# An attention-plus-MLP kernel: score tiles of three and two heads in turn, VectorE's scores beside them, shared PSUM banks, filler matmuls

## The chip, the cores and the metric

One core of a Trainium2 chip. Times are device microseconds (us) of one execution. A run of one core is called slow when it lies over 1.5% above the fastest run of the same kernel in its session. The other runs are called fast. "Half clock" below is a granted TensorE clock of 0.50 in the records; full is 1.00.

## The reference, cut to what matters

Sequence 2048, width 512, 32 heads of 16. The result gates two branches that read the same input `x`:

```python
g = sigmoid((x * gate_w).sum(-1, keepdims=True))
q, k, v = heads(x @ wqkv)                        # (cut) 32 heads of 16
p = softmax((q @ k.T) * 16 ** -0.5)              # 2048 x 2048 for each head
a = merge(p @ v) @ wo
h = gelu(layernorm(x) @ w1)                      # (cut) then shifted along the sequence in four quarters
x1 = x + shifted(h) @ w2
b = x1 + gelu(layernorm(x1) @ w3) @ w4           # 512 -> 1792 -> 512
out = g * a + (1 - g) * b
```

The exponentials dominate: 32 heads of 2048 x 2048. With keys on the partitions this is 2048 blocks of 128 x 512.

## The kernel before

The kernel walks 32 groups: four chunks `c` of 512 queries by eight sets `g` of four heads. A group has 16 key tiles `kt` of 128 keys. In 13 of them ScalarE takes the exp. In the other three (`DKT`) VectorE approximates it: one op per head turns a score into integer bits (`kb`), and four adds make shifted copies (`sj`), which enter the value product as bf16. I call one such key tile a VectorE unit.

Contraction is over 32 rows, so a score matmul takes one of four row groups of the array, and matmuls on different row groups overlap ("row" passes: in the trace of before, at half clock, two together take 0.61 us, as long as one full-array matmul). Value products use four column groups ("col" passes: four together take 0.62 us). Everything else uses the full array.

```python
DKT = (4, 9, 14)
T_ALL = 880.0                                     # sets how fast the schedule hands out the side work
...                                               # (cut)
ps_act = tile_pool(name="ps_act", bufs=2, space=PSUM)    # 2 x 2 banks: exp's scores
ps_dve = tile_pool(name="ps_dve", bufs=1, space=PSUM)    # 1 bank: VectorE's scores
ps_acc = tile_pool(name="ps_acc", bufs=1, space=PSUM)    # 1 bank: the group's value product
ps_gen = tile_pool(name="ps_gen", bufs=2, space=PSUM)    # 2 banks: projections, MLP
...
def qk_a(n):                                      # two heads of one key tile
    c, g, kt, hf = a_tiles[n]
    stage[n] = st = ps_act.tile([P, 1024], F32, tag="sa", name="sa")
    for j in range(2):
        scores(st[:, j * 512:(j + 1) * 512], c, g, kt, 2 * hf + j)

def exp_a(n):
    pts[n] = pt = ptpool.tile([P, 1024], BF16, tag="pt", name="pt")
    nc.scalar.activation(out=pt[:], in_=stage.pop(n)[:], func=ACT.Exp, scale=LN2 / 128.0)
...
def qk_d(h):                                      # one head for VectorE
    st[h] = ps_dve.tile([P, 512], F32, tag="sd", name="sd")
    scores(st[h][:], c, g, kt, h)

def k_op(h):
    nc.vector.tensor_scalar(out=sj[0][:, h * 512:(h + 1) * 512], in0=st.pop(h)[:],
                            scalar1=KB, scalar2=0.0, op0=ALU.add, op1=ALU.max)
```

A list scheduler in the kernel's Python fixes the order on every engine before the program exists. It weighs exps first and puts projections, VectorE units and MLP into the gaps by due times.

The softmax here doesn't subtract the row's maximum and nothing guards it: scores larger than these inputs give would overflow.

Of the kernel before, what the change touches and what calls it, by code (L numbers as in the profile page):

```python
# [26 lines left out]
POOL_J = ()  # L27
DKT = (4, 9, 14)
PTB = 7
KPB = 2  # L30
SPB = 5
T_ALL = 880.0
# [33 lines left out]
class Task:  # L66
    def __init__(self, sched, engine, cost, fn, deps, due, mode, take, give, lat, qk):
        self.sched, self.engine, self.cost, self.fn, self.due, self.mode = sched, engine, cost, fn, due, mode
        self.take, self.give, self.lat, self.qk = take, give, lat, qk
        self.deps, self.done, self.blocked = deps, Event(), 0  # L70
        for d in deps:
            if d.t is None:
                d.waiters.append(self)
                self.blocked += 1
        if not self.blocked:
            sched.ready[engine].append(self)
        sched.left += 1


class Scheduler:  # L80
# [9 lines left out]
    TOL = 0.12  # L90

    def __init__(self, t0):
        self.ready = {e: [] for e in self.LAT}
        self.free = {e: t0 for e in self.LAT}
        self.mode, self.left = None, 0
        self.busy = {e: 0.0 for e in self.LAT}

    def add(self, engine, cost, fn, deps=(), due=0.0, mode=None, take=(), give=(), lat=None, qk=False):
        t = Task(self, engine, cost, fn, list(deps), due, mode, take, give, self.LAT[engine] if lat is None else lat, qk)
        return t.done  # L100
# [12 lines left out]
    def pick(self, e):  # L113
        t, best = self.free[e], None
        cands = []
        qk = None
        for k in self.ready[e]:
            s = self.start_of(k, t)
            if s is None:
                continue  # L120
            if k.qk:
                if qk is None or k.due < qk[1].due:
                    qk = (s, k)
            else:
                cands.append((s, k))
        if e == "PE" and qk is not None:
            limit = qk[0] + self.TOL
            cands = [(s, k) for s, k in cands if s + k.cost + (self.SWITCH if k.mode != self.mode else 0.0) <= limit]
            cands.append(qk)
        if not cands:  # L130
            return None
# [3 lines left out]

    def run(self):
        while self.left:
            picks = [(p[0], e, p[1]) for e in self.LAT if self.ready[e] and (p := self.pick(e)) is not None]
            s, e, k = min(picks, key=lambda p: p[0])
            self.emit(s, e, k)  # L140

    def emit(self, s, e, k):
        self.ready[e].remove(k)
        for r in k.take:
            r.take()
        cost = k.cost
        if e == "PE" and k.mode != self.mode:
            cost += self.SWITCH
            self.mode = k.mode
        self.now = s  # L150
        k.fn()
        self.left -= 1
        self.busy[e] += cost
        self.free[e] = s + cost
        for r in k.give:
            r.give(s + cost + k.lat)
        k.done.set(s + cost + k.lat)
# [3 lines left out]
def kernel(  # L161
# [28 lines left out]
    AKT = [t for t in range(NT) if t not in DKT]  # L190
    ND, NA = len(DKT), len(AKT)

# [6 lines left out]
    ps_act = ctx.enter_context(tc.tile_pool(name="ps_act", bufs=2, space=bass.MemoryType.PSUM))  # L199
    ps_dve = ctx.enter_context(tc.tile_pool(name="ps_dve", bufs=1, space=bass.MemoryType.PSUM))  # L200
# [13 lines left out]
    NVA, NVD = NA * H * VW, ND * H * VW  # L214
# [12 lines left out]
    junk = work.tile([P, D], BF16, tag="ot", name="junk")  # L227
    djc = const.tile([P, max(1, len(POOL_J))], I32, name="djc")

# [26 lines left out]
    for k, j in enumerate(POOL_J):  # L256
        nc.vector.memset(djc[:, k:k + 1].bitcast(I16), DJ[j])

    T0 = 13.0
    sc = Scheduler(T0)  # L260
    add = sc.add
    gen_s, acc_s, act_s, dve_s = Slots(2), Slots(1), Slots(2), Slots(1)
    pt_s, k_s, sj_s, q_s, xn_s, xnT_s = Slots(PTB), Slots(KPB), Slots(SPB), Slots(2), Slots(2), Slots(1)
    accsb_s, bcs_s, oTg_s, oT_s, ot_s = Slots(2), Slots(1), Slots(1), Slots(2), Slots(2)
    MM, DV, DV4, DV2 = 0.216, 0.69, 0.43, 0.43

    def gen_tile(dt=F32):
        return ps_gen.tile([P, 512], dt, tag="gen", name="gen")


    def mm_group(pairs, evacs, deps, due, n=512, ev_due=0.5, take0=()):
# [8 lines left out]
        for i, (a, b) in enumerate(pairs):  # L280
            prev = add("PE", MM * n / 512, lambda i=i, a=a, b=b: mm(i, a, b), list(deps) + ([prev] if prev else []) if i == 0 else [prev],
                       due, "full", take=(gen_s,) + tuple(take0) if i == 0 else (), lat=None if i == len(pairs) - 1 else 0.0)
        for i, (cost, fn, take, give) in enumerate(evacs):
            prev = add("DVE", cost, lambda fn=fn: fn(box["ps"]), [prev], due + ev_due, take=take,
                       give=tuple(give) + ((gen_s,) if i == len(evacs) - 1 else ()))
        return prev

    def transposes(src, dst, deps, due, give=()):
        box = {}

        def pe():
            box["ps"] = ps = gen_tile(BF16)
            for kt in range(KT):
                nc.tensor.transpose(ps[:, kt * P:(kt + 1) * P], src()[:, kt * P:(kt + 1) * P], ident[:])  # L294

        e = add("PE", 0.25, pe, deps, due, "full", take=(gen_s,), give=give)
        return add("DVE", DV2, lambda: nc.vector.tensor_copy(out=dst(), in_=box["ps"][:].rearrange("p (k t) -> p k t", k=KT)),
                   [e], due + 0.5, give=(gen_s,))


    PER = (T_ALL - T0 - 15.0) / (NCH * NG * 2 * NA)

    def when(c, g, kt=0.0):
        return T0 + ((c * NG + g) * 2 * NA + 2 * NA * kt / NT) * PER
# [7 lines left out]
    k_ev = {(0, 0): Event(T0)}  # L312
    q_ev = {(0, 0): Event(T0)}
# [4 lines left out]
    def project_k(g, c, due):  # L318
        k_ev[(g, c)] = mm_group(
            [(wkv[:, 0, kt, P * g:P * g + P], xT[:, kt, c * 512:(c + 1) * 512]) for kt in range(KT)],  # L320
            [(DV, lambda ps: nc.vector.tensor_copy(out=kT[g][:, c * 512:(c + 1) * 512], in_=ps[:]), (), ())],
            xT_ev[4 * c:4 * c + 4], due)

    def q_evac(g, c, ps, par):
        if par == 0:
            qm[(g, c)] = work.tile([P, 2, 512], BF16, tag="qT", name="qT")
        nc.vector.tensor_scalar(out=qm[(g, c)][:, par, :], in0=ps[:], scalar1=qmask[:, par:par + 1], scalar2=None,  # L327
                                op0=ALU.mult)

    def project_q(g, c, due):  # L330
        q_ev[(g, c)] = mm_group(
            [(wq[:, kt, P * g:P * g + P], xT[:, kt, c * 512:(c + 1) * 512]) for kt in range(KT)],
            [(DV, lambda ps: q_evac(g, c, ps, 0), (), ()), (DV, lambda ps: q_evac(g, c, ps, 1), (), ())],
            xT_ev[4 * c:4 * c + 4], due, take0=(q_s,))

    def v_evac(t, h0, nh, j, ps):
        src = ps[:, 0:nh * DH].rearrange("p (h d) -> p h d", h=nh)
        if t in AKT:
            nc.vector.tensor_copy(out=vpA[:, AKT.index(t), h0:h0 + nh, 1:VW], in_=src)
            return  # L340
        dst = vpD[j][:, DKT.index(t), h0:h0 + nh, :]
        nc.vector.tensor_scalar(out=dst[:, :, 1:VW], in0=src, scalar1=CJ[j], scalar2=None, op0=ALU.mult)

    def project_v(t, half, due):
        h0, nh = 16 * half, 16
        v_ev[(t, half)] = mm_group(
            [(xT[:, kt, t * P:(t + 1) * P], wkv[:, 1, kt, h0 * DH:(h0 + nh) * DH]) for kt in range(KT)],
            [(0.43, lambda ps, j=j: v_evac(t, h0, nh, j, ps), (), ()) for j in range(1 if t in AKT else NJ)],
            xT_ev[t:t + 1], due, n=nh * DH)

    for c in range(1, NCH):
# [3 lines left out]
    for t in range(NT):  # L355
        project_v(t, 1, when(0, 4) - 60.0 + 3.0 * t)
    for c in range(NCH):
# [8 lines left out]
    cg = [(c, g) for c in range(NCH) for g in range(NG)]  # L366
    a_tiles = [(c, g, kt, hf) for c, g in cg for kt in AKT for hf in range(2)]
    nA = len(a_tiles)
    stage, pts = {}, {}
    accs = {}  # L370
    left = {k: NA + ND * NJ for k in cg}
    q_use = {}
    for c, g in cg:
        q_use[(g // 2, c)] = q_use.get((g // 2, c), 0) + NA * 2 + ND * 4
# [11 lines left out]
    d_next = {"n": 0}  # L386
    d_units = []

    def qk_a(n):
        c, g, kt, hf = a_tiles[n]  # L390
        stage[n] = st = ps_act.tile([P, 1024], F32, tag="sa", name="sa")
        for j in range(2):
            scores(st[:, j * 512:(j + 1) * 512], c, g, kt, 2 * hf + j)
        q_done(g // 2, c)

    def exp_a(n):
        pts[n] = pt = ptpool.tile([P, 1024], BF16, tag="pt", name="pt")
        nc.scalar.activation(out=pt[:], in_=stage.pop(n)[:], func=ACT.Exp, scale=LN2 / 128.0)  # L398
# [61 lines left out]
    for n, (c, g, kt, hf) in enumerate(a_tiles):  # L460
        t = T0 + n * PER
        e = add("PE", 0.226, lambda n=n: qk_a(n), [k_ev[(g // 2, kt // 4)], q_ev[(g // 2, c)]], n, "row", take=(act_s,), qk=True)
        exp_ev.append(add("ACT", 0.9625, lambda n=n: exp_a(n), [e], t, take=(pt_s,), give=(act_s,)))
        if hf == 1:
            pv_ev[(c, g)].append(add(
                "PE", MM, lambda n=n, k=(c, g), kt=kt: pv(k, kt, AKT.index(kt) * H * VW, lambda i: (
                    pts[n - 1 + i // 2][:, (i % 2) * 512:(i % 2 + 1) * 512])),
                exp_ev[-2:] + [v_ev[(kt, g // 4)]] + pv_ev[(c, g)][:1], t + 3.0, "col",
                take=(acc_s,) if kt == AKT[0] else (), give=(pt_s, pt_s), lat=-MM if kt == AKT[0] else None))
# [4 lines left out]
    for c, g in cg:  # L474
        for x, kt in enumerate(DKT):
            t0 = when(c, g, (x + 0.3) * NT / ND) - LEADT
# [5 lines left out]
            def qk_d(h, c=c, g=g, kt=kt, st=st):  # L482
                st[h] = ps_dve.tile([P, 512], F32, tag="sd", name="sd")
# [3 lines left out]
            def k_op(h, st=st, sj=sj):  # L487
                if h == 0:
# [4 lines left out]
            def add_op(j, sj=sj):  # L493
                sj[j] = spool.tile([P, 2048], I16, tag="sj", name="sj")
                if j in POOL_J:
                    nc.gpsimd.tensor_add(sj[j][:].bitcast(I32), sj[0][:].bitcast(I32),
# [284 lines left out]
```

## Time and profile before

| | before |
|---|---|
| median, runs | 974.91 us; 973.31 to 982.2 (4 runs) |
| profiled span | 978.9 us, mean clock 0.906 |
| busy: TensorE, ScalarE, VectorE | 890.6, 832.9, 727.8 us |

From the page of before, part 1 (busy us, share of the span, instructions) and three lines of part 2 (the span in 40 slices; `PEclk` is the granted clock in tenths):

```profile
PE 890.6 (91%) x6632; PEld 262.7 (27%) x6730; DVE 727.8 (74%) x1286; ACT 832.9 (85%) x906; POOL 57.5 (6%) x42
...
DVE  2898899989998883468878477887656888845652
ACT  1647877899998986699999899999889999979990
...
PEclk7888999999999985599999699999689999959985
```

No engine is saturated from end to end. ScalarE has holes early, and drops to 6 to 8 tenths wherever `PEclk` falls to 5 or 6. The next answer is of the same trace in 20-us windows; its columns are the window, its length, the busy us (and instructions) of TensorE, its weight loads, VectorE, ScalarE and GpSimd, then clock, DMA share and GB/s:

```profile
core 0: us, PE busy (x) PEld busy (x) DVE busy (x) ACT busy (x) POOL busy (x), PEclk, DMA share, GB/s
40.00:60.00 20.00, 16.85 (x117) 7.17 (x113) 17.64 (x44) 5.82 (x6) 0.00 (x0) 0.71 0.00 1
60.00:80.00 20.00, 17.53 (x122) 5.93 (x123) 16.84 (x45) 11.80 (x13) 0.00 (x0) 0.83 0.01 2
360.00:380.00 20.00, 18.90 (x86) 3.45 (x86) 7.03 (x13) 13.62 (x15) 0.00 (x0) 0.50 0.01 2
380.00:400.00 20.00, 19.53 (x103) 3.37 (x100) 7.88 (x13) 12.90 (x13) 1.26 (x1) 0.50 0.05 17
420.00:440.00 20.00, 19.25 (x158) 5.75 (x159) 15.13 (x25) 20.00 (x23) 1.28 (x1) 1.00 0.06 18
```

There are three regimes. At 40–80 VectorE is 84 to 88% busy and ScalarE starves. At 360–400 the clock is 0.50, TensorE is 95 to 98% busy and ScalarE gets 13 to 14 of 20 us. At 420 the clock is full and ScalarE runs without a hole. ScalarE's timeline in the second and third regime (start, length, instructions merged, and in brackets the idle time before and what ended it):

```profile
350.10 1.28 ACT L644 ACT_TABLE_LOAD   x1
351.39 7.40 ACT L644 ACTIVATE g2T<-g2T 128x512 bf16<-128x512 bf16 x14
358.81 1.28 ACT L398 ACT_TABLE_LOAD   x1
...
366.95 1.02 ACT L398 ACTIVATE pt<-sa 128x1024 bf16<-128x1024 f32 x1 [0.48 <-PE sa L383]
368.58 1.02 ACT L398 ACTIVATE pt<-sa 128x1024 bf16<-128x1024 f32 x1 [0.60 <-PE sa L383]
...
417.54 33.51 ACT L398 ACTIVATE pt<-sa 128x1024 bf16<-128x1024 f32 x36 [0.22 <-PE sa L383]
```

Gelu (`g2T`) and its two table loads occupy 10 us. Then exps come about 1.5 us apart, nearly all singly and most of them waiting for `PE sa`, until 417; after that 36 follow in 33.51 us. TensorE in the slow regime:

```profile
366.25 0.61 PE L383 MATMUL sa<-qT,kT 32*128 32x512 bf16 x2
366.78 0.62 PE L408 MATMUL acc<-pt,vp 128*32 128x512 bf16 x4
367.33 0.61 PE L612 MATMUL gen<-w,g2T 128*128 128x512 bf16 x1
367.87 0.61 PE L383 MATMUL sa<-qT,kT 32*128 32x512 bf16 x2
368.41 1.03 PE L612 MATMUL gen<-w,g2T 128*128 128x512 bf16 x2
369.38 0.61 PE L383 MATMUL sa<-qT,kT 32*128 32x512 bf16 x2
```

Each pass of a new kind starts 0.54 us after the last, and a second of the same kind 0.42 us. From one score tile to the next it takes 1.5 to 1.6 us, more than the 0.93 us of an exp. ScalarE's waits in total (us, times, longest):

```profile
ACT pt L398 <- PE acc L408: 54.7, 38, 7.1
...
ACT pt L398 <- PE sa L383: 44.3, 64, 4.7
```

### The profile page before, as it was taken

How to read it: one execution, taken by the hardware profiler on the slowest of the kernel's cores; microseconds unless marked ns; L12 is line 12 of the kernel's file. 1: busy time of each engine (PE TensorE's matmuls, PEld its weight loads, DVE VectorE, ACT ScalarE, POOL GpSimd, SP SyncE). 2: the span in 40 equal slices, each digit the busy share in tenths (PEclk: the TensorE clock that was granted, in tenths of full speed). 3: DMA queues.
4: the chain of work that ended last, by engine and by line, in shares of the span. 5: the costliest groups of instructions: out<-in, count | busy, mean ns of one | idle time of the engine just before them, and what ended most of it. 6: DMA issues, size and time to landing. Idle time of an engine off the chain costs nothing.

```text
span 978.9 us, 17077 instructions
## 1 busy us (share of the span) xinstructions
PE 890.6 (91%) x6632; PEld 262.7 (27%) x6730; DVE 727.8 (74%) x1286; ACT 832.9 (85%) x906; POOL 57.5 (6%) x42
## 2 busy tenths in 40 slices
PE   4879999999999989999999999999899999899982
PEld 1332333322232221122222222222222222212220
DVE  2898899989998883468878477887656888845652
ACT  1647877899998986699999899999889999979990
POOL 5000000000000000000000000000000000000000
PEclk7888999999999985599999699999689999959985
DMA  7000000020020000001000000000000100000001
GB/s 220 1 1 16 15 3 15 15 90 15 14 90 10 16 10 15 1 16 37 15 15 16 15 13 22 31 15 14 5 15 15 32 20 17 12 4 16 15 16 36
DMA packets 27953, 23.52 MB, mean 24 GB/s; under 512 B 12000, under 2 KB 23136, under 8 KB 27872
## 3 DMA queue, kind: packets, MB, share of 16 engines
q1 hardware_dynamic: 27072, 21.64, 7.1%
q8 instruction: 52, 0.85, 0.4%
q10 hardware_dynamic: 800, 0.79, 0.2%
q14 instruction: 29, 0.24, 0.1%
HBM read 17.69 MB, written 2.62 MB: 21 GB/s over the span
## 4 chain that ended last, share of the span: by engine, by line
PE 50%; ACT 30%; issue 9%; DVE 9%; DMA 1%; SPq 0%; POOLq 0%; ACTq 0%; DVEq 0%
ACT pt L398 26%; PE sa L383 16%; PE acc L408 14%; PE gen L612 7%; PE gen L595 5%; PE sd L383 4%; DVE sj L499 4%; PE gen L277 3%; ACT g2T L644 2%; DVE kb L490 2%; PE gen L294 1%; ACT hT L644 1%; DVE qT L327 1%; ACT L398 1%; DMA bcs<-rd 0%
## 5 line engine op out<-in xcount | busy, mean ns | idle before, releaser
L398 ACT ACTIVATE pt<-sa 128x1024 bf16<-128x1024 f32 x832 | 780.7, 1062 | 104.0 <-PE acc L408 54.7
L383 PE MATMUL sa<-qT,kT 32*128 32x512 bf16 x1664 | 345.5, 403 | 32.4 <-ACT pt L398 25.3
L490 DVE TENSOR_SCALAR kb<-sd 128x512 int16<-128x512 f32 x384 | 263.2, 685 | 125.0 <-PE sd L383 112.8
L499 DVE TENSOR_SCALAR sj<-kb 128x2048 int16<-128x2048 int16 x384 | 264.2, 726 | 1.9
L383 PEld LDWEIGHTS <-kT 32*128 32x128 bf16 x2048 | 103.4, 92 | 332.4 <-issue 321.8
L408 PE MATMUL acc<-pt,vp 128*32 128x512 bf16 x1664 | 166.4, 408 | 0.3 <-ACT pt L398 0.3
L383 PE MATMUL sd<-qT,kT 32*128 32x512 bf16 x384 | 152.4, 397 | 7.4 <-DVE kb L490 5.4
L408 PE MATMUL acc<-sj,vp 128*32 128x512 bf16 x1536 | 149.0, 414 | 5.2 <-DVE sj L499 4.6
L408 PEld LDWEIGHTS <-vp 128*32 128x32 bf16 x3584 | 75.9, 96 | 181.8 <-issue 173.5
L441 POOL TENSOR_TENSOR oTg<-accsb,bcs 128x512 bf16<-128x512 f32 x32 | 43.9, 1372 | 907.3 <-DMA bcs<-rd 645.7
L595 PE MATMUL gen<-xnT,w 128*128 128x512 bf16 x252 | 81.0, 385 | 1.6 <-issue 1.4
L612 PE MATMUL gen<-w,g2T 128*128 128x512 bf16 x194 | 76.7, 472 | 3.1 <-issue 3.1
L602 DVE CAST g2T<-gen 128x512 bf16<-128x512 f32 x56 | 38.4, 686 | 15.0 <-PE gen L595 12.2
L420 DVE COPY accsb<-acc 128x512 f32<-128x512 f32 x32 | 22.0, 689 | 27.5 <-issue 20.4
L408 PE MATMUL acc<-kb,vp 128*32 128x512 bf16 x384 | 40.5, 413 | 0.3 <-issue 0.3
L595 PEld LDWEIGHTS <-w 128*128 128x128 bf16 x288 | 21.8, 97 | 49.8 <-issue 44.7
L612 PE MATMUL gen<-wo,oT 128*128 128x512 bf16 x58 | 20.1, 434 | 15.2 <-DMA oT<-oTg 14.6
L612 PEld LDWEIGHTS <-g2T 128*128 128x128 bf16 x224 | 17.1, 103 | 46.6 <-issue 42.8
L644 ACT ACTIVATE g2T<-g2T 128x512 bf16<-128x512 bf16 x56 | 29.6, 616 | 0.0
L719 DVE TENSOR_TENSOR x_sb<-x_sb,gen 128x512 bf16<-128x512 bf16 x16 | 11.0, 686 | 24.6 <-PE gen L612 21.2
L327 DVE TENSOR_SCALAR qT<-gen,qmask 128x512 bf16<-128x512 f32 x32 | 23.7, 744 | 4.2 <-PE gen L743 3.0
L687 DVE TENSOR_TENSOR dd<-gen,x_sb 128x512 f32<-128x512 f32 x16 | 11.0, 688 | 17.1 <-PE gen L612 17.0
(68 smaller groups left out, 336.9 us busy)
## 6 DMA issues: line engine op xcount, KB each, us to landing
bcs<-rd SPq DMA_DIRECT2D x32, 256.0 KB
w<-in_B_w_dram SPq DMA_DIRECT2D x2, 1792.0 KB
oT<-oTg SPq DMA_DIRECT2D x128, 16.0 KB, 1.8
out_dram<-ot SPq DMA_DIRECT2D x16, 128.0 KB, 2.3
x_sb<-in_A_x_dram SPq DMA_DIRECT2D x3, 512.0 KB
w<-in_B_w_dram SPq DMA_DIRECT2D x2, 512.0 KB
wq<-in_A_wqkv_dram SPq DMA_DIRECT2D x1, 512.0 KB
wkv<-in_A_wqkv_dram ACTq DMA_DIRECT2D x1, 512.0 KB, 7.2
```

Of the source, the lines that this page charges most:

```text
L277: nc.tensor.matmul(box["ps"][:, 0:n], lhsT=a, rhs=b, start=(i == 0), stop=(i == len(pairs) - 1))
L327: nc.vector.tensor_scalar(out=qm[(g, c)][:, par, :], in0=ps[:], scalar1=qmask[:, par:par + 1], scalar2=None, op0=ALU.mult)
L383: nc.tensor.matmul(dst, lhsT=kT[g // 2][r:r + 32, kt * P:(kt + 1) * P], rhs=qm[(g // 2, c)][r:r + 32, g % 2, :], start=True, stop=True, ti ...
L398: nc.scalar.activation(out=pt[:], in_=stage.pop(n)[:], func=ACT.Exp, scale=LN2 / 128.0)
L408: nc.tensor.matmul(accs[k][32 * i:32 * i + 32, :], lhsT=vp[:, v:v + 32], rhs=parts(i), start=first, stop=left[k] == 0, skip_group_check=Tr ...
L441: nc.gpsimd.tensor_tensor(out=box["o"][:], in0=box["a"][:], in1=box["b"][:], op=ALU.mult)
L490: nc.vector.tensor_scalar(out=sj[0][:, h * 512:(h + 1) * 512], in0=st.pop(h)[:], scalar1=KB, scalar2=0.0, op0=ALU.add, op1=ALU.max)
L499: nc.vector.tensor_scalar(out=sj[j][:], in0=sj[0][:], scalar1=float(DJ[j]), scalar2=None, op0=ALU.add)
L595: nc.tensor.matmul(outs["ps"][:], lhsT=w()[:, i, m * P:(m + 1) * P], rhs=box["xnT"][:, i, :], start=(i == 0), stop=(i == KT - 1))
L602: return e, add("DVE", DV, lambda: nc.vector.tensor_copy(out=dst(), in_=outs["ps"][:]), [e], at + 0.5, give=(gen_s,))
L612: nc.tensor.matmul(outs["ps"][:], lhsT=a, rhs=b, start=(i == 0), stop=(i == len(pairs) - 1))
L644: nc.scalar.activation(out=t[:, m, n0:n1], in_=t[:, m, n0:n1], func=ACT.Gelu_apprx_tanh)
```

## The change

The intent, read from the edit:

- Score tiles hold three and two heads in turn (3 + 2 banks), so fewer exps and fewer row passes.
- VectorE's scores lose their bank and use the two general ones. A score matmul for VectorE is put right behind a score tile that leaves its row group free.
- The first chunk has fewer VectorE units (`DN`), and until 90 us of the schedule's time ScalarE may take PSUM evacuations (copies of matmul results out of PSUM).
- When the schedule sees TensorE idle and lightly loaded, a matmul on a constant tile fills the gap, to hold the clock.

```diff
-DKT = (4, 9, 14)
-PTB = 7
+DKT = (3, 8, 13)
+PTB = 3                                  # of each of two sizes
-SPB = 5
-T_ALL = 880.0
+SPB = 4
+T_ALL = 860.0
+ALT_UNTIL = 90.0
+DN = ((0, 2, 2, 2, 2, 3, 3, 3), (3,) * 8, (3,) * 8, (3,) * 8)
...                                       (cut: scheduler)
+            if min(s, pe) >= t + 0.36 and self.recent(t + 0.3) < self.LOAD and self.idle(t):
+                self.busy_pe(t, 0.216, "full", 512)      # filler matmul
...
+        if k.rows:                       # after a score tile: VectorE scores on row groups it leaves free
+            used = set(k.rows)
+            while True:
+                m = [x for x in self.ready["PE"] if x.side and not used & set(x.rows) ...]
...                                       (cut: pools)
-    ps_act = ... bufs=2
-    ps_dve = ... bufs=1
+    ps_act = ... bufs=1                  # one buffer for each of two tags
...
+    tiles, i = [], 0
+    while i < len(heads):
+        n = 3 - len(tiles) % 2
+        tiles.append(heads[i:i + n])
+        i += n
     def qk_a(n):
-        stage[n] = st = ps_act.tile([P, 1024], F32, tag="sa", name="sa")
+        stage[n] = st = ps_act.tile([P, (3 - n % 2) * 512], F32, tag=f"sa{n % 2}", name="sa")
...
-                st[h] = ps_dve.tile([P, 512], F32, tag="sd", name="sd")
+                st[h] = gen_tile()
...                                       (cut: evacuations on either engine, scaled V copies as late tasks of their own)
```

The instruction order of the two programs, counted (a pass is a set of matmuls of one kind on different row or column groups; a switch is a change between row, col and full):

| | before | after |
|---|---|---|
| exps | 832 of 1024 | 338 of 1536, 339 of 1024 |
| row passes, col passes | 1023, 896 | 801, 868 |
| switches | 1909 | 1606 |
| `kb` and `sj` ops on VectorE | 384, 384 | 356, 356 |
| filler matmuls | 0 | 9, the first after head 1670 of 1692 |

## The prediction

> **What bounds it now.** Three things in turn (busy time by 20-us stretches). (1) Up to about 200 us VectorE is 88 to 96% busy and exp starves: ScalarE ran 11.8 of 20 us in 60–80 and 5.8 in 40–60, with 7.1 and 6.2 us idle runs that the waits put on `PE acc`; behind those stand late evacuations, and the clock reads 0.71 in 40–60. (2) In the good stretches (420–540, 720–800) ScalarE is 100% busy and exp is the limit: twelve 1024-wide exps took 11.22 us, 0.935 us each. (3) After each gelu block (two 1.28 us table loads and 7.4 us of gelu) TensorE falls to half clock and stays there: clock 0.50 in 360–400, 0.58 in 400–420, and again after 540, 700 and 860. There exps come one at a time, about 1.5 us apart: ScalarE 13–15 of 20 us, VectorE 7, TensorE 97%: TensorE bounds them.
>
> Exp itself needs 832 × 0.935 = 778 us. With the start (22 us), five non-exp blocks of about 10 us and the tail after the last exp (27 us) that is 877 us of 979 (profiled; 975 timed). The other 102 us are stalls: about 47 before the first quarter of exp ends (near 274 us), about 55 later.
>
> **What changes, costed.**
> - Exp: 832 instructions become 338 of 1536 and 339 of 1024. The Trainium skill, "ScalarE: Activation LUTs" (What ACT_TABLE_LOAD costs), gives 0.833 ns per element more; with the trace's 0.935 us I estimate 1.362 us for three heads. 338 × 1.362 + 339 × 0.935 = 777 us: nothing gained, because seven of 96 VectorE units are dropped and their 28 heads go to ScalarE. ScalarE also takes some eight evacuations (about 5 us).
> - TensorE: from the instruction order, row-tiled score passes fall from 1023 to 801, column quads from 896 to 868, mode switches from 1909 to 1606. The trace shows 0.216 us between passes of one mode and 0.32 at a switch, so about 53 + 30 us less TensorE time, from about 800 to 720 us warm. Per 208 heads, before needs about 91–111 us against exp's 97; after 82–94. TensorE gets slack, and in the half-clock stretches, where it is the limit, some 12% more speed.
> - VectorE: 28 `kb` (0.685) and 28 `sj` (0.726) fewer, eight evacuations fewer, 30 more V copies of 0.42: about −30 us, nearly all in the first quarter, where it is critical.
> - VectorE's scores lose their own bank and share the two general ones: some new waits.
> - Fillers: only nine, all in the last 25 heads and the tail. They cannot stop the half-clock stretches after gelu. Small.
>
> **Prediction.** Floor about 890 us (more heads and evacuations in the first quarter). Early stalls 47 → about 15; later stalls 55 → about 35, the half-clock stretches staying but shorter. 940 profiled, **936 us** timed; 8 in 10 between 915 and 960. Faster by over 2%: 0.80, within 2%: 0.17, slower: 0.03.
>
> **Right or wrong, in the profile.** 1536-wide exps 1.36 us apart, ScalarE busy total about unchanged (833 ± 10 us); TensorE busy falls; no 6–7 us ScalarE idles at 40–70 us; ScalarE above 85% in 40–200 us; half-clock stretches still follow the gelu blocks ("TensorE: Matmul & The Clock Gate", Part 1: an idle window drops the clock to half; here it stays low while TensorE is 97% busy), but with denser exp in them.
>
> **What would make it wrong.** TensorE, now less busy, falls cold more often, or for longer, than before. Shared banks: long MLP accumulations hold one general bank, VectorE's scores wait, and later units pile up at group ends. Three exp buffers of each size block when a value product runs late. MLP work slips and lengthens the tail. On the upside, if the half-clock locks vanish, 915.

## The result

Ratios are the mean time of one kernel's fast runs over that of the other's fast runs of the same rounds, so they are not quite the ratios of the medians quoted beside them.

The changed kernel took **933.51 us** median (931.13 to 935.43, 4 runs) against 974.91, a ratio of 0.956 (95% interval 0.9505 to 0.9616). The output is correct. The profiled run (933.7 us, clock 0.921) is fast.

The page of the changed kernel, the same lines:

```profile
PE 824.3 (88%) x6651; PEld 254.9 (27%) x6651; DVE 686.6 (74%) x1228; ACT 828.5 (89%) x759; POOL 58.7 (6%) x42
...
DVE  1996687878985887778688678888666888857732
ACT  1689996999978899999889999999999999999980
...
PEclk7799999999986997998898999999799999979897
```

The same regimes in windows:

```profile
core 0: us, PE busy (x) PEld busy (x) DVE busy (x) ACT busy (x) POOL busy (x), PEclk, DMA share, GB/s
40.00:60.00 20.00, 16.27 (x144) 7.72 (x141) 18.39 (x55) 16.73 (x16) 0.00 (x0) 1.00 0.00 1
60.00:80.00 20.00, 18.31 (x164) 7.58 (x164) 16.87 (x47) 18.25 (x17) 0.00 (x0) 1.00 0.02 3
140.00:160.00 20.00, 17.72 (x127) 5.92 (x130) 15.96 (x32) 12.82 (x12) 0.00 (x0) 0.91 0.02 5
340.00:360.00 20.00, 16.75 (x104) 4.36 (x102) 16.76 (x27) 19.08 (x25) 1.59 (x1) 0.74 0.05 18
360.00:380.00 20.00, 19.96 (x172) 5.62 (x172) 13.75 (x23) 19.88 (x18) 1.46 (x1) 1.00 0.06 16
380.00:400.00 20.00, 19.48 (x184) 5.73 (x177) 14.40 (x25) 20.00 (x19) 0.57 (x1) 1.00 0.06 18
```

At 40–80 ScalarE has 35 of 40 us instead of 18. The clock still drops around the gelu block (0.74 in 340–360), but 360–400 runs at full clock and ScalarE is never short. ScalarE's timeline there:

```profile
345.47 1.28 ACT L767 ACT_TABLE_LOAD   x1
346.76 7.38 ACT L767 ACTIVATE g2T<-g2T 128x512 bf16<-128x512 bf16 x14
354.17 1.28 ACT L503 ACT_TABLE_LOAD   x1
355.46 3.28 ACT L503 ACTIVATE pt<-sa 128x1024 bf16<-128x1024 f32 x3
359.61 82.19 ACT L503 ACTIVATE pt<-sa 128x1536 bf16<-128x1536 f32 x72 [0.87 <-PE gen L480]
```

Four microseconds after the gelu block exps run on: 72 of them in 82.19 us, 2.28 us for each pair of sizes. A merged line names only its first form. ScalarE's waits have halved:

```profile
ACT pt L503 <- PE acc L517: 22.5, 15, 4.5
...
ACT pt L503 <- PE sa L480: 19.0, 24, 2.4
```

Where the 45 us of the two profiled spans come from, on ScalarE's account (the span is start + exp + other blocks + tail + idle):

| us | before | after |
|---|---|---|
| first exp starts | 22.5 | 23.6 |
| exp, busy | 780.7 | 772.0 |
| idle before the first chunk's exps end (274, 264 us) | 48 | 25 |
| idle from there to the last exp | 52 | 34 |
| last exp to the end | 26 | 26 |

The idle rows are sums over 1-us windows from 23 us on. The rest is gelu, table loads and, after, some 4 us of evacuations. So 41 us of the 45 are idle time gone, 23 early and 18 late.

Length of the half-clock stretch that begins within 22 us of the first table load of each of the five gelu blocks (1-us windows with a clock below 0.75), with ScalarE's idle time in it:

| us | gelu 1 | gelu 2 | gelu 3 | gelu 4 | gelu 5 |
|---|---|---|---|---|---|
| before | none | 58 (20) | 17 (4) | 24 (7) | 28 (8) |
| after | 6 (0) | 10 (1) | 7 (0) | 14 (1) | 13 (2) |

### The profile page after: what moved, and what is told of

Read it like the earlier page. It is cut to its first block, busy times and chain, and to the rows that moved or that the text cites. A ratio compares the mean times of both kernels' runs of the same rounds, so it can differ in the third digit from the quotient of the medians.

```text
span 933.7 us, 16666 instructions
## 1 busy us (share of the span) xinstructions
PE 824.3 (88%) x6651; PEld 254.9 (27%) x6651; DVE 686.6 (74%) x1228; ACT 828.5 (89%) x759; POOL 58.7 (6%) x42
## 4 chain that ended last, share of the span: by engine, by line
PE 39%; ACT 37%; issue 14%; DVE 6%; DMA 2%; POOL 2%; SPq 0%; POOLq 0%; ACTq 0%; DVEq 0%
ACT pt L503 32%; PE acc L517 11%; PE sa L480 11%; PE gen L735 6%; PE gen L718 4%; PE gen L353 4%; ACT g2T L767 3%; PE gen L480 2%; DVE sj L617 2%; POOL vp L311 2%; DMA bcs<-rd 1%; DVE kb L612 1%; PE gen L372 1%; DVE bnst L657 1%; ACT L503 1%
## 5 line engine op out<-in xcount | busy, mean ns | idle before, releaser
L503 ACT ACTIVATE pt<-sa 128x1536 bf16<-128x1536 f32 (+1 forms) x677 | 772.0, 1309 | 46.6 <-PE acc L517 22.5
L480 PE MATMUL sa<-qT,kT 32*128 32x512 bf16 x1692 | 274.1, 396 | 52.9 <-ACT pt L503 48.1
L612 DVE TENSOR_SCALAR kb<-gen 128x512 int16<-128x512 f32 x356 | 237.8, 681 | 104.6 <-PE gen L480 103.4
L617 DVE TENSOR_SCALAR sj<-kb 128x2048 int16<-128x2048 int16 x356 | 237.1, 705 | 4.1 <-PE acc L517 2.6
L480 PEld LDWEIGHTS <-kT 32*128 32x128 bf16 x2048 | 92.8, 91 | 313.3 <-issue 305.8
L480 PE MATMUL gen<-qT,kT 32*128 32x512 bf16 x356 | 136.9, 400 | 8.3 <-DVE kb L612 8.1
L517 PE MATMUL acc<-sj,vp 128*32 128x512 bf16 x1424 | 130.2, 405 | 5.4 <-DVE sj L617 4.9
L718 PE MATMUL gen<-xnT,w 128*128 128x512 bf16 x288 | 87.8, 394 | 0.6
L735 PE MATMUL gen<-w,g2T 128*128 128x512 bf16 x224 | 71.4, 414 | 0.4 <-DVE kb L612 0.3
L353 PE MATMUL gen<-wkv,xT 128*128 128x256 bf16 x152 | 26.9, 286 | 3.0 <-DVE kb L612 2.2
```

The lines of the kernel that those rows point to most:

```text
L353: nc.tensor.matmul(box["ps"][:, 0:n], lhsT=a, rhs=b, start=(i == 0), stop=(i == len(pairs) - 1))
L480: nc.tensor.matmul(dst, lhsT=kT[g // 2][r:r + 32, kt * P:(kt + 1) * P], rhs=qm[(g // 2, c)][r:r + 32, g % 2, :], start=True, stop=True, ti ...
L503: nc.scalar.activation(out=pt[:, 0:m], in_=stage.pop(n)[:, 0:m], func=ACT.Exp, scale=LN2 / 128.0)
L517: nc.tensor.matmul(accs[k][32 * i:32 * i + 32, :], lhsT=vp[:, v:v + 32], rhs=parts(i), start=first, stop=left[k] == 0, skip_group_check=Tr ...
L617: nc.vector.tensor_scalar(out=sj[j][:], in0=sj[0][:], scalar1=float(DJ[j]), scalar2=None, op0=ALU.add)
L718: nc.tensor.matmul(outs["ps"][:], lhsT=w()[:, i, m * P:(m + 1) * P], rhs=box["xnT"][:, i, :], start=(i == 0), stop=(i == KT - 1))
```

## The experiments

Theory A: TensorE's passes and switches were the load that held it at half clock for so long; the wider tiles relieve it, and the late idle time goes with the passes. Theory B: fewer exps, or the fifth score bank, are what count. For the early part: theory C, VectorE was overloaded and dropping units (with evacuations moved to ScalarE) cures it; its rival is that the tiles cure that too. All experiments start from the changed kernel unless said otherwise. All ran on one chip, in three sessions of four kernels. In each session the kernel before was run again, and its spread there is wide: 966.84 to 1033.51, 974.64 to 1027.69 and 954.31 to 1019.31. The third session has only one fast run of before, so e9 to e12 have no ratio. The time of before follows its mean clock, from 0.938 at 954.31 to 0.842 at 1033.51. I use its fast runs only, and compare mostly with e5, which is the changed kernel but for the nine fillers and ran on this chip (934.0 mean of 4 fast runs).

**e1_tiles22: two heads in every tile**

```diff
-        n = 3 - len(tiles) % 2
+        n = 2
-PTB = 3
+PTB = 4          # and [P, 1024] for both tile tags
```

> The changed kernel with all score tiles of two heads (846 exps of 1024 instead of 338 of 1536 and 339 of 1024), still sharing the spare banks. At about 0.93 us each the exps need some 788 us instead of 771: if only the exp instruction count counts, 17 us slower, about 950. From the instruction order the row passes go from 801 to 922 and the mode switches from 1606 to 1860, about 50 us more TensorE time: if TensorE's relief is what shortened the stalls, the stalls grow too (58 us to 75-90), half-clock stretches after the gelu blocks come back, and the time is 965 to 980.

Median 986.28; the fast runs' mean is 984.9 (3 runs, clocks 0.881 to 0.892), ratio to before 1.015 (1.003 to 1.027). That is 51 us over e5, and 47 over e2 of its own session: the whole gain is gone. This run also leaves a bank unused: its two tiles take four score banks instead of five, and VectorE's scores still share the general ones. The exps are 794.2 us busy, 22 us more than after. The profile fell in a slow run (1003.6 us), and it shows the long stretches again, 34, 76 and 34 us after gelu 3 to 5 (columns as before):

```profile
700.00:720.00 20.00, 20.00 (x73) 3.58 (x72) 8.54 (x14) 14.22 (x15) 0.00 (x0) 0.50 0.00 1
720.00:740.00 20.00, 20.00 (x105) 3.47 (x104) 5.80 (x10) 13.00 (x14) 1.27 (x1) 0.50 0.06 18
780.00:800.00 20.00, 19.22 (x152) 5.70 (x150) 15.20 (x25) 20.00 (x23) 0.00 (x0) 1.00 0.09 29
```

It is the picture of before at 360–400. Idle from 350 us on is 58 us against 19 after. But idle from 23 to 200 us is 30, near the 23 after. In this profile most of the early gain is there without the wide tiles and the late one is not. The fast runs of e1 have no profile, but their mean clocks point the same way. Where the clock reads 0.50 or 1.00, the time at half clock is 2 x (1 - mean clock) x span, so I estimate 210 to 235 us of it in them, and 145 to 155 in e5.

**e2_noside: no score placed beside a tile on purpose**

```diff
-                        mode="row", load=128, take=(gen_s,), rows=(h,), side=True)
+                        mode="row", load=128, take=(gen_s,), rows=(h,))
```

> The changed kernel, but VectorE's score matmuls are no longer placed beside a score tile on the free row group; they are ordinary tasks in the gaps. Row passes 801 to 887, switches about the same (1616): some 19 us more TensorE time. If TensorE binds only in short stretches, 3 to 10 us slower (937 to 944), with longer half-clock stretches; if TensorE's slack is ample everywhere, within 2 us.

936.33 us median (935.46 to 942.81), fast mean 937.7, 3.7 us over e5; the sessions differ, so I call it small rather than settled. The stretches after the gelu blocks are 10, 17, 10, 21 and 14 us, somewhat longer than after. It fits 86 more row passes costing little.

**e3_dn3: three VectorE units in every group**

```diff
-DN = ((0, 2, 2, 2, 2, 3, 3, 3), (3,) * 8, (3,) * 8, (3,) * 8)
+DN = ((3,) * 8, (3,) * 8, (3,) * 8, (3,) * 8)
-FIRST_D = (0, 1)
+FIRST_D = (0, 0)
```

> The changed kernel with three VectorE units in every group (24 instead of 17 in the first quarter), so 28 heads go from ScalarE (-12.7 us of exp) to VectorE (+39 us). If VectorE's overload bounded the first quarter, the early stalls grow by 25 to 35 us and the time is 945 to 955, with VectorE over 90% busy in 40 to 200 us. If it did not, the time falls by about 10 us, to 923.

947.92 us median, fast mean 944.5 (3 runs), 10.6 us over e5, although ScalarE has 28 heads less. Idle from 23 to 200 us rises from 23 to 49; idle after 350 is 17, as low as after. Theory C holds for the sign and the place. VectorE is not over 90% busy throughout, as I expected: it shows 75 to 91% in the windows from 40 to 200. Most of its idle time there ends with a matmul, so it also waits for TensorE. The two extremes, in which ScalarE is far below the 18.25 and 18.18 us that it has after:

```profile
60.00:80.00 20.00, 16.53 (x106) 5.47 (x104) 14.93 (x39) 13.11 (x16) 0.00 (x0) 0.73 0.00 1
160.00:180.00 20.00, 16.82 (x134) 6.32 (x131) 18.16 (x38) 11.27 (x10) 0.81 (x1) 1.00 0.02 5
```

`FIRST_D` also sets when the scaled V copies of the first groups are due, so this run undoes the units and the placing of their copies together.

**e4_noalt: no evacuations on ScalarE**

```diff
-ALT_UNTIL = 90.0
+ALT_UNTIL = 0.0
```

> The changed kernel without the eight evacuations on ScalarE before 90 us. ScalarE loses about 4 us of work, VectorE gains about 5 us. If the early evacuations are on the critical path, 3 to 8 us slower, with ScalarE idle longer in 25 to 65 us; otherwise within 2 us of 933.

929.21 us median (926.46 to 931.45), mean 929.1: 0.5% below e5, not slower. The evacuations on ScalarE are no part of the gain. Where the changed kernel runs four of them, between 30.5 and 41.2 us, the trace of e4 has a ScalarE hole of 11.19 us; the next exp starts at 41.2 us with them and at 42.2 without.

**e5_nofill: without the filler matmuls**

```diff
     def idle(t):
-        if (a := gen_s.at()) is None or a > t:
-            return False
+        return False
```

> The changed kernel without the nine matmuls on the constant tile; it also serves as the changed kernel on this chip. They all stand in the last 25 heads and the tail, so within 3 us of 933 whatever the theory; if they mattered, the last 30 us of the trace show a lower clock and the tail after the last exp is over 30 us instead of 26.5.

933.94 us median (931.86 to 936.21); ratio to before 0.952 (0.944 to 0.960). The fillers do nothing measurable. They sit at the very end of the order.

**e6_extra1 and e7_extraA: the passes given back, the tiles kept**

Every third score tile computes scores twice into the same bank, so the results stay right. e6 repeats one head, e7 all heads of the tile.

```diff
             scores(st[:, j * 512:(j + 1) * 512], c, g, kt, h)
             q_done(g // 2, c)
+        if n % 3 == 0:
+            scores(st[:, j * 512:(j + 1) * 512], c, g, kt, h)          # e6
+            # e7: the same for every (j, head) of tiles[n]
```

> The changed kernel, same order, but every third score tile computes its last head a second time into the same bank: 226 more matmuls, each a pass of its own that drives one row group of four (row passes 801 to 1015, switches the same, exps and buffers the same). That gives back about 49 us of TensorE time at full clock, what e1_tiles22 gave back in passes and switches. If TensorE's passes were what the wider tiles relieved, about 20 to 35 us slower (953 to 968), with long half-clock stretches after the gelu blocks again; if the gain came from fewer exps or from the fifth score bank alone, within 8 us.

> As e6_extra1, but the same tiles repeat all their heads (two or three row groups at once): the same number of extra passes (1027 row passes) and the same TensorE time, but two to three times the work done by the array in them. If only TensorE time counts, the same as e6_extra1 within 5 us. If the clock depends on how much of the array is driven per unit of time, the half-clock stretches end sooner, the mean clock is higher and it is 8 to 20 us faster than e6_extra1.

e6: 958.5 us median (946.67 to 961.81), fast mean 951.2 (2 runs). e7: 953.44 (948.46 to 961.54), fast mean 954.2 (4 runs). They are 17 and 20 us over e5, and the same within their spread. So TensorE time costs something even with wide tiles: about 20 us for some 220 passes. (Profile against profile, e7 is 26 us longer than e5: 16 us are idle time, and 10 us are added exp busy time, 781.2 against 771.5.) How much of the array a repeated pass drives made no difference that these runs show. But the long stretches did not come back. After the gelu blocks the half clock lasts 7, 10, 7, 14 and 13 us in e7 (a fast run), and 7 to 17 in e6. This refutes half of theory A: the number of passes alone does not make the stretches long. Here is e7 where before was at half clock for 58 us, in 20-us windows:

```profile
360.00:380.00 20.00, 19.03 (x126) 4.36 (x121) 13.41 (x24) 17.41 (x18) 0.00 (x0) 0.75 0.01 2
380.00:400.00 20.00, 20.00 (x177) 5.63 (x173) 13.12 (x21) 19.40 (x18) 1.61 (x1) 1.00 0.06 18
```

**e8_tiles22_own: two-head tiles, and a bank of its own for VectorE's scores**

```diff
-                st[h] = gen_tile()
+                st[h] = ps_dve.tile([P, 512], F32, tag="sd", name="sd")    # on top of e1_tiles22; (cut) its pool and slot
```

> e1_tiles22 with VectorE's scores in a bank of their own again (eight banks in all, as before), which is the old bank layout with the rest of the change. If sharing the two general banks cost something, 5 to 15 us faster than e1_tiles22 (983 in its fast runs); but the order has more row passes (962) and switches (1985), so if TensorE time decides, the same or 5 to 15 us slower.

Median 975.84, from 949.17 to 996.65, with one fast run; no ratio could be formed. The profile (a slow run, 968.9 us) has stretches of 31, 17, 27 and 68 us after gelu 1 to 4. There is none after gelu 5, and idle from 23 to 200 us is 22. Whether sharing the banks costs anything is left open. The one fast run, 949.17 us, is below all three fast runs of before in that session (974.64 to 986.51), so e1 may owe part of its loss to the bank that it leaves unused; one run does not settle it. The slow profile does show the long stretches and the wide spread of two-head tiles a third time, beside before and e1.

**e9_before_gelufill: the kernel before, with fillers inside the gelu blocks**

```diff
+        if e == "PE" and s < self.hot and s >= self.last + EVERY and k.done_group and self.idle(s + cost):
+            ...                          # one matmul on a constant tile, general bank; self.hot is set by gelu
```

> The kernel before, plus matmuls on a constant tile in the gaps of the gelu blocks alone (5 to 13 in each block, 48 in all, into general banks that are free there). If the long half-clock stretches begin because TensorE idles in the gelu block, and cost what I read from the trace (about 25 to 35 us of ScalarE idle), then they do not begin, the mean clock rises above 0.93, the time falls to 940 to 955 and the runs spread less. If the clock falls anyway, or the stretches begin for another reason, the time stays within 1% of before.

Median 988.95 (953.63 to 1010.91) against 996.22 in the same session: no gain that can be told from the spread, and the spread is as wide as ever. Each has one fast run, and they agree (953.63 and 954.31). The profile, a slow run, is mixed. After gelu 1, 2 and 5 there is no half clock at all and after gelu 3 only 10 us, but after gelu 4 it lasts 81 us, and there are new early stretches (23 to 54, 81 to 118 us). The experiment does not settle that idling in the gelu block starts the stretches.

**e10_gelufill and e12_best: the changed kernel with such fillers; e12 also without evacuations on ScalarE**

```diff
                 st[h] = gen_tile()
+                for _ in range(NJUNK if sc.now < sc.hot else 0):           # NJUNK = 1
+                    nc.tensor.matmul(st[h][:], lhsT=junk[:, 0:P], rhs=junk[:], start=True, stop=True)
```

> The changed kernel, plus one matmul on the constant tile ahead of each of VectorE's score matmuls that falls into a gelu block (35 in all, same bank, overwritten). Its half-clock stretches after the gelu blocks are 7 to 14 us each; without them ScalarE should lose 1 to 3 us less per block: 5 to 12 us faster than 933. If TensorE's idling there is not what lowers the clock, the same or up to 5 us slower.

> The changed kernel without evacuations on ScalarE (which was 929 by itself) and with the matmuls on the constant tile in the gelu blocks: 918 to 925 if the two gains add up, 929 if the fill does nothing.

e10: 928.27 us median (927.76 to 934.93), mean 929.8, mean clock 0.932 to 0.947 where e5 had 0.917 to 0.921. e12: 929.33 (927.63 to 934.13), mean 930.1. The fillers raise the clock, and the time falls by some 4 us against e5 of another session. In the profile of e10 the stretches after the gelu blocks are 7, 7, 7, 0 and 7 us (e5: 6, 10, 7, 14 and 13), and in e12 they are 0, 0, 14, 7 and 10 (e4: 7, 13, 10, 10 and 10). So in the changed kernel they are shorter in sum with filled gelu blocks, as expected if TensorE's idling there helps to start them. The two small gains do not add up. e4, e10 and e12 are all near 929, half a per cent below the changed kernel, and cannot be told apart.

**e11_tilesonly: the changed kernel with all parts but the tiles and shared banks undone, as far as switches allow**

It is the changed kernel with the edits of e2, e3, e4 and e5 together, and with the old `DKT` and `T_ALL`. It is not quite the kernel before with new tiles: the rewritten scheduler stays (score tiles in a fixed order, scaled V copies as tasks of their own, four `sj` buffers instead of five).

> The kernel before with the tiles of three and two heads and the shared banks, and next to nothing else: three VectorE units in every group at the old places, no evacuations on ScalarE, no matmuls on the constant tile, no score beside a tile on purpose, pace as before. If the wider tiles carry the change: 940 to 950 (933 plus 11 for the early units, plus 3 for the side placement, minus 4 for the evacuations). If the parts need one another, 960 or more.

978.53 us (976.45 to 983.46), all four runs fast: I expected 940 to 950. The windows show where:

```profile
40.00:60.00 20.00, 15.28 (x125) 6.14 (x123) 19.03 (x52) 5.66 (x6) 0.00 (x0) 0.83 0.00 1
60.00:80.00 20.00, 16.74 (x109) 5.56 (x110) 16.79 (x44) 11.48 (x10) 0.00 (x0) 0.83 0.00 1
400.00:420.00 20.00, 18.77 (x156) 5.56 (x154) 9.75 (x16) 20.00 (x19) 0.26 (x1) 1.00 0.02 4
```

After gelu 2 the clock is back in 6 us, and ScalarE is full from 400 on. But early it starves worse than before: 5.66 of 20 us in 40–60, and 62 us idle from 23 to 200 (before 46, e3 49, after 23). One hole is 9.98 us long, ended by `PE sa`; in that hole VectorE works almost without a pause through statistics, four `sj` adds, five scaled V copies and other evacuations, and TensorE waits for it three times. It also has 29 us of idle after 350 us (e2 28, after 19). Singly, e2 to e5 cost 3.7, 10.6, −4.9 and 0 us, about 9 together; e11 costs 45 over e5. `DKT` and `T_ALL` were not tried by themselves, so whether they or the interplay make up the other 36 is open. So is what the rewritten scheduler does by itself: no run has it without the rest.

## Why the prediction was right

The measured 933.51 us lies 2.5 us from the 936 foretold. That it is so close is partly luck: the floor was 15 us too high and the stalls 9 us too low. Point by point:

- **"Exp ... 777 us: nothing gained".** Right: 772.0 busy. The estimate of 1.362 us for a 1536-wide exp came from the Trainium skill, "ScalarE: Activation LUTs" (What ACT_TABLE_LOAD costs), which gives 0.833 ns per element. The trace agrees: 2.28 us a pair, less the 0.93 us of the 1024-wide one, is 1.35. "Nothing gained" holds for the sum with its 28 more heads. With two-head tiles the same heads take 846 exps, 788 us at the 0.93 us of one in a row (794 in the slow profile of e1), so the wider tiles do save about 16.
- **"Floor about 890 us".** Wrong, by an error of my own. The listed parts (22 + 777 + 50 + 5 + 27) add up to 881; I had counted the extra heads twice. The measured floor is 934 less 59 of idle, 875. The slip was offset in part by stalls that were larger than I said.
- **"Early stalls 47 → about 15".** The place was right, the size too hopeful: 48 to 25. Between 30.5 and 41.2 us ScalarE still runs only four evacuations, and 140–160 has ScalarE at 12.82 of 20 us, so "above 85% in 40–200 us" failed there and, narrowly, in 40–60. The idle runs of 6 to 7 us at 40–70 are gone, as foretold (the longest is 2.25). The cause given was VectorE. e3 supports it (idle 23 to 49 when the units come back) and the profile of e1, a slow run, has most of the early gain without wide tiles (30). The evacuations on ScalarE, which I had counted as part of it, are not (e4).
- **"Later stalls 55 → about 35".** 52 to 34. "The half-clock stretches staying but shorter": 58, 17, 24 and 28 us became 10, 7, 14 and 13.
- **"In the half-clock stretches ... some 12% more speed".** The reason for the shorter stretches was given as fewer passes. This is the step that held only in part. At half clock before ran 37 exp tiles of two heads in 57.4 us (360.1 to 417.5), 0.78 us a head. The changed kernel in its longest half-clock stretch (274.7 to 294.7, at a group's end rather than after gelu) got 32 heads into 20 us, 0.63 a head, so it is faster there, by about a fifth. But passes are only worth some 20 us (e6, e7), and giving them back did not bring the long stretches back. What goes with long stretches is the two-head tile; why is not shown. The four profiles with it (before, e1, e8, e9) have stretches of up to 58, 76, 68 and 81 us after a gelu block; the ten with tiles of three and two heads stay at 21 or less. Of the four, only before is a fast run, so the firm comparison is its 58, 17, 24 and 28 us against the fast profiles of the changed kernel, e2, e3, e4, e5, e7, e10, e11 and e12. Between the wider tiles' fewer switches (1606 against 1860 in e1), their fewer exps and the fifth score bank, the runs do not decide. Nor does a two-head kernel fall into long stretches in every run. By the estimate under e1, the fastest run of before (954.31 us, clock 0.938) had some 120 us of half clock in all, fewer than e5, and it is still 20 us slower than e5. That is about the early gain of 23; so how much the change gains late depends on how much half clock the run of before has.
- **"Fillers ... Small".** Right: none (e5).
- **"VectorE's scores ... share the two general ones: some new waits".** Open. e8 could not tell.

As to the size of each part, undone singly: the tile width 51 us (with a bank left unused), the early units 10.6, the side placement about 4, the evacuations −5, the fillers 0. These are not additive. Without the tiles and with a bank idle the rest gains nothing (e1, 984.9 against 970.4 for the fast runs of before); with the old bank layout that is open (e8). The tiles without most of the rest end at 979 (e11). In the profiles each half goes with one kind of idle time: e11 keeps the early one (62 us), e1 the late one (58).

## What to carry to other kernels

Account for the limiting engine as floor plus idle time, split the idle time by stage, and ask of each part of a change which stage it can reach; here two parts went with two different stages. Check that the parts of a floor really add up: mine did not, and only a second error hid it. When a kernel's runs spread by several per cent along its mean clock, look for stretches where the clock stays low although TensorE looks fully busy. Here they stayed short in all ten profiles with tiles of three and two heads, while fillers in the gelu blocks of before gained nothing that could be told from the spread.

## What the Trainium skill lacked or had wrong

- "TensorE: Matmul & The Clock Gate" (Part 1) has the full clock return after one busy window of about 3.4 us. Here TensorE was 95% busy by the profile while the clock stayed at 0.50 for 58 us (before, 359 to 417), and 99% busy in 76 us of half clock in e1 (a slow run). So busy time as the profile shows it did not bring the full clock back; the page (its caveats on clock records aside) does not explain this, and does not say how row-tiled passes count. Its table of two states, half and full, agrees with the 2-us windows, which show 0.50 or 1.00 except where a window straddles a change (before and after, around the second gelu block).
- "TensorEngine Tiling (Array Packing)" (Key Properties) says that changing the tiling mode drains TensorE, without a figure. At full clock the starts lie 0.32 us apart at a change and 0.22 within a mode; at half clock 0.54 and 0.42 (before). About 0.1 us for each change, and this kernel has 1600 to 1900.
- No page has it that the time at half clock can differ so much between runs of one kernel that the total spreads by 8%: the kernel before ran from 954 to 1034 us with mean clocks of 0.938 to 0.842.
